# Batch one's forward twiddle tables formed on chip, with full-width forward matmuls and one product per pair

## The chip, the cores and the metric

The kernel runs on one core of one Trainium2 chip. The metric is the device time of one execution in microseconds; for the kernel before it is the median of three runs. The engines are TensorE (PE, with weight loads shown apart as PEld), VectorE (DVE), ScalarE (ACT), GpSimd (POOL) and SyncE (SP). DMAs are issued from the queues of POOL and SP here.

## What is computed

The reference filters a sequence in the frequency domain and sends the result through a small two-layer network with PReLU:

```python
X = np.fft.rfft(x, axis=1)                       # x: 8 batches x 3008 x 256
Y = X * (filt_r + 1j * filt_i)[None]             # 1505 frequencies x 256
y = np.fft.irfft(Y, n=3008, axis=1).reshape(24064, 256)
h = y @ w_in                                     # 256 -> 2048
g = np.maximum(h, 0) + alpha * np.minimum(h, 0)
out = g @ w_out                                  # 2048 -> 256
```

## The kernel before

The FFT of length 3008 is split as 47 x 64. Per batch there are four stages: A (47-point transforms, `piece_a`), B (twiddle and 64-point transform for each of 24 frequencies k1, two to a pair kp, `piece_b`), C (the inverse of B, `piece_c`) and D (the inverse of A, `piece_d`). Between B and C the spectrum is multiplied by the filter. The network works on blocks of up to 512 tokens: `up` (L421 matmuls, ACT copies to `gtb` in L427, DVE does min, multiply and add in L430 and L431) and `down` (L440, stored from L403). All is issued in one hand-written order: a dictionary `plan` says at which step of the blocks' loop each piece of a later batch's transform stands (16 steps a block, from step 0 at the first `up`). Engines work through their queues in order.

Batches 1 to 7 are transformed beside the blocks of earlier batches. Batch 0 (class `First`) comes first, and nothing else can fill TensorE meanwhile. This head is what the change touches:

- The x rows of batch 0 are loaded in four chunks of two DMAs (L139, POOL's queue, with a cast from float32 to float16). `piece_a` runs 16 pieces, four to a chunk; each one's eviction to `am`, a part of `gtb`, alternates between ACT and DVE (L245, L248). `warm` issues matmuls whose results nobody reads.
- The constants follow on POOL's queue in four groups of six frequencies: the forward table `twf_s` (L332), the filter `filt_s` (real and imaginary part, each in a rising and a falling run: four DMAs, L144 and L148), the inverse table `twi_s` (L336) and its crossed copy `twx_s` (L338), which lies in the last three slots of `gtb`. For the first group DVE makes `twx_s` from `twi_s` (`cross`, L354 and L355). Then come `win_s`, `wout_s` and x of batch 1.
- `turn_at` transposes a pair of frequencies into `at` (L278). `piece_b` does eight half-width matmuls (L288) into two banks of a `psH` buffer: one bank has real and imaginary part in one order, the other crossed. DVE multiplies each with the filter (L292, L293) to `uu` and `ww`. `piece_c` sums both through `twi_s` and `twx_s` (L305, L306), ACT evicts to `v`. The order per pair is C of kp, transposes of kp + 3, B of kp + 2.
- `piece_t` (L317) and `piece_d` (L238) finish the batch, its first quarter ahead of the first `up`.

From batch 1 on, `piece_b` takes a 128-wide weight from `twf_s` (L197), DVE multiplies with `filts_s` and `filt_s` (L200, L201), and a DMA adds the halves (L203). For this `filts_s` and `filt_s` have to hold other halves than in batch 0: a DMA after the head (L378), four DVE negations at steps 17, 20, 23 and 26 (`neg`, L481) and a DMA at step 29 bring them there.

PSUM has two `psH` buffers of two banks, two `psO` buffers and two single banks (`psF`), which a string of digits, `BANKS`, deals out.

Of the kernel before, what the change touches and what calls it, by code (L numbers as in the profile page):

```python
# [10 lines left out]
FP16 = mybir.dt.float16  # L11
FP32 = mybir.dt.float32

NFFT = 3008
N1 = 47
N2 = 64
NK1 = 24
D = 256
# [14 lines left out]
AF = mybir.ActivationFunctionType  # L33
OP = mybir.AluOpType


def _build_consts():

    s1 = np.arange(N1)
    s2 = np.arange(N2)
    k1 = np.arange(NK1)
    p = np.arange(64)
    k2 = np.where(p < 32, p, 95 - p)
    g = np.where(p < 32, 1.0, -1.0)

    a1 = 2 * np.pi * np.outer(s1, k1) / N1  # L50
    wf1 = np.zeros((2 * N1, 96))
    wi3 = np.zeros((96, 2 * N1))
    scale = np.where(k1 == 0, 1.0, 2.0) / NFFT
    for h in range(2):
        r = slice(h * N1, h * N1 + N1)
        wf1[r, h * 48 : h * 48 + NK1] = np.cos(a1)
        wf1[r, h * 48 + NK1 : h * 48 + 48] = -np.sin(a1)
        wi3[h * NK1 : h * NK1 + NK1, r] = (np.cos(a1) * scale).T
        wi3[48 + h * NK1 : 48 + h * NK1 + NK1, r] = (-np.sin(a1) * scale).T

    kk = k1[:, None] + 47 * k2[None, :]
    ang = 2 * np.pi * s2[:, None, None] * kk[None, :, :] / NFFT
    c, s = np.cos(ang), np.sin(ang)
    twf = np.empty((128, NK1, 128))
    twf[:64, :, :64], twf[64:, :, :64] = c, s
    twf[:64, :, 64:], twf[64:, :, 64:] = -s * g, c * g
    ec, es = c.transpose(2, 1, 0), s.transpose(2, 1, 0)
    gp = g[:, None, None]
    twi = np.empty((128, NK1, 128))
    twi[:64, :, :64], twi[:64, :, 64:] = ec, es  # L70
    twi[64:, :, :64], twi[64:, :, 64:] = -es * gp, ec * gp
    return wf1, wi3, twf, twi


@with_exitstack
def kernel(
# [8 lines left out]
    out: bass.AP,  # L85
):
    nc = tc.nc
    wf1_np, wi3_np, twf_np, twi_np = _build_consts()
    wf1_d = nc.inline_tensor(wf1_np.astype(np.float16), name="c_wf1")
    wi3_d = nc.inline_tensor(wi3_np.astype(np.float16), name="c_wi3")  # L90
    twf_d = nc.inline_tensor(twf_np.astype(np.float16), name="c_twf")
    twi_d = nc.inline_tensor(twi_np.astype(np.float16), name="c_twi")
    twx_np = np.concatenate([twi_np[64:], -twi_np[:64]])
    twx_d = nc.inline_tensor(twx_np.astype(np.float16), name="c_twx")
    id_d = nc.inline_tensor(np.eye(128, dtype=np.float16), name="c_id")
    wfx_np = wf1_np.reshape(2 * N1, 2, 2, NK1).transpose(0, 3, 2, 1).reshape(2 * N1, 96)
    wfx_d = nc.inline_tensor(np.ascontiguousarray(wfx_np).astype(np.float16), name="c_wfx")
# [15 lines left out]

    wf1_s = konst.tile([2 * N1, 96], FP16, name="wf1_s")
    wi3_s = konst.tile([96, 2 * N1], FP16, name="wi3_s")
    twf_s = konst.tile([128, NK1, 128], FP16, name="twf_s")
    twi_s = konst.tile([128, NK1, 128], FP16, name="twi_s")
    filt_s = konst.tile([128, NK1, D], FP16, name="filt_s")
    filts_s = konst.tile([128, NK1, D], FP16, name="filts_s")
    al16 = konst.tile([16, 128], FP32, name="al16")  # L120
# [40 lines left out]
    class Fft:  # L161
# [31 lines left out]
        def piece_b(self, kp):  # L193
            px = bank().rearrange("p (k d) -> p k d", k=2)
            for kh in range(2):
                k1 = 2 * kp + kh
                nc.tensor.matmul(px[:, kh], twf_s[:, k1], self.at[:, k1], start=True, stop=True)  # L197
            uu = p_uw.tile([128, 2, D], FP16, name="uu", bufs=4)
            ww = p_uw.tile([128, 2, D], FP16, name="ww")
            nc.vector.tensor_mul(ww, px, filts_s[:, 2 * kp : 2 * kp + 2])  # L200
            nc.vector.tensor_mul(uu, px, filt_s[:, 2 * kp : 2 * kp + 2])  # L201
            for o in (0, 64):
                nc.gpsimd.dma_start(out=uu[o : o + 64], in_=ww[64 - o : 128 - o], accum_op=OP.add)  # L203
            self.uw[kp] = (uu,)
# [48 lines left out]
    class First(Fft):  # L253
# [26 lines left out]

        def piece_b(self, kp):
            hp = psH.tile([128, 2, 512], FP32, name="hps")
            px, pz = (hp[:, i].rearrange("p (k d) -> p k d", k=2) for i in range(2))
            for i, ps in enumerate((px, pz)):
                for kh in range(2):
                    k1 = 2 * kp + kh
                    for o in (0, 64):
                        nc.tensor.matmul(ps[o : o + 64, kh], twf_s[:, k1, 64 * i : 64 * i + 64],  # L288
                                         self.at[:, k1], start=True, stop=True)
            uu = p_uw.tile([128, 2, D], FP16, name="uu", bufs=4)  # L290
            ww = p_uw.tile([128, 2, D], FP16, name="ww")
            nc.vector.tensor_mul(uu, px, filt_s[:, 2 * kp : 2 * kp + 2])  # L292
            nc.vector.tensor_mul(ww, pz, filt_s[:, 2 * kp : 2 * kp + 2])  # L293
            self.uw[kp] = uu, ww

        def piece_c(self, kp, evict):
            uu, ww = self.uw.pop(kp)
# [12 lines left out]
        def piece_t(self, i, evict, wide=False):  # L310
# [6 lines left out]
                    nc.tensor.matmul(pt[0:96, o : o + 128], m[:, 8 * f + s // 4, :, s % 4], id16, start=True, stop=True)  # L317
            evict(self.zt[:, 2 * i : 2 * i + 2].rearrange("p a d -> p (a d)"), pt[0:96])

    nc.sync.dma_start(out=id16, in_=id_d.ap())  # L320
    nc.sync.dma_start(out=wfx_s, in_=wfx_d.ap())
    xc = {(0, c): load_x(0, c) for c in range(4)}
    f0 = First()
# [1 line left out]
    nc.sync.dma_start(out=wf1_s, in_=wf1_d.ap())  # L325
    nc.sync.dma_start(out=wi3_s, in_=wi3_d.ap())
    make_identity(nc, id32)
    for g in range(4):
        ka, kb = 6 * g, 6 * g + 6
        kc = slice(ka, 24 if g == 2 else kb)  # L330
        if g < 3:
            nc.gpsimd.dma_start(out=twf_s[:, kc], in_=twf_d.ap()[:, kc])  # L332
        load_filt(filt_s, 0, filt_r, ka, kb)
        load_filt(filt_s, 64, filt_i, ka, kb)
        if g < 3:
            nc.gpsimd.dma_start(out=twi_s[:, kc], in_=twi_d.ap()[:, kc])  # L336
        if g > 0:
            nc.gpsimd.dma_start(out=twx_s[:, ka:kb], in_=twx_d.ap()[:, ka:kb])  # L338
    for kt in range(2):
        nc.gpsimd.dma_start(out=win_s[:, kt], in_=moe_w_in[kt * 128 : (kt + 1) * 128])  # L340
    for q in range(2):
        nc.gpsimd.dma_start(
            out=wout_s[:, 8 * q : 8 * q + 8],
            in_=moe_w_out[1024 * q : 1024 * q + 1024].rearrange("(j p) d -> p j d", p=128))
    for c in range(4):
        xc[(1, c)] = load_x(1, c)

    def warm(n):
        pw = psO.tile([128, 2, D], FP32, name="op")
        for _ in range(n):  # L350
            nc.tensor.matmul(pw[:, 0, 0:128], id16, id16, start=True, stop=True)

    def cross(ka, kb):
        nc.vector.tensor_copy(twx_s[0:64, ka:kb], twi_s[64:128, ka:kb])  # L354
        nc.vector.tensor_scalar(twx_s[64:128, ka:kb], twi_s[0:64, ka:kb], -1.0, None, OP.mult)  # L355

    warm(36)
    for i in range(16):
        f0.piece_a(i, both[i % 2], i % 2 == 1)
        if i % 4 == 3:  # L360
            warm((16, 6, 5, 8)[i // 4])
    alp = psO.tile([128, 2, D], FP32, name="op")
    nc.tensor.transpose(alp[:, 0, 0:16], al16, id32)
    nc.vector.tensor_copy(al_s, alp[:, 0, 0:16])
# [1 line left out]
    f0.turn_at(0, on_act)  # L366
    f0.turn_at(1, on_dve)
    f0.piece_b(0)
    cross(0, 6)
    f0.turn_at(2, on_act)  # L370
    f0.piece_b(1)
    for kp in range(12):
        f0.piece_c(kp, on_act)
        if kp < 9:
            f0.turn_at(kp + 3, on_act)
        if kp < 10:
            f0.piece_b(kp + 2)
    nc.gpsimd.dma_start(out=filts_s[0:64], in_=filt_s[64:128])  # L378
    warm(8)
    for i in range(4):  # L380
        f0.piece_t(i, both[i % 2], i % 2 == 1)
# [7 lines left out]
    for p in range(NB // 2):  # L389
        t = 0  # L390
# [60 lines left out]
    def put(step, fn, *args):  # L451
        plan.setdefault(step, []).append((fn, args))
# [25 lines left out]
            put(d0 + gap * i, f0.piece_d, 4 * g + i, evs[i % len(evs)])  # L478

    def neg(ka, kb):  # L480
        nc.vector.tensor_scalar(filts_s[64:128, ka:kb], filt_s[64:128, ka:kb], -1.0, None, OP.mult)  # L481

    for i in range(4):
        put(17 + 3 * i, neg, 6 * i, 6 * i + 6)
    put(29, lambda: nc.gpsimd.dma_start(out=filt_s[64:128], in_=filt_s[0:64]))
    plan_fft(1, 16, 1, 32, 40, 3, 0, 6, 92, 4, (20, 24, 74, 75))
    plan_fft(2, 66, 2, 97, 109, 4.5, 8, 12, 187, 4, (110, 114, 118, 122))
    for b in range(3, NB):
        p = 96 * (b - 1)
        f = Fft(b)  # L490
# [63 lines left out]
```

## Time and profile before

| what | us |
|---|---|
| median of three runs (796.51 to 797.36) | 796.84 |
| the profiled execution's own time | 795.65 |
| its span, first to last instruction | 793.9 |
| PE / DVE / ACT / POOL busy | 775.0 / 621.2 / 596.9 / 193.2 |
| first x chunk used by `piece_a` | 6.33 |
| last x chunk used | 12.80 |
| first product with the filter starts | 16.34 |
| last of them ends | 33.25 |
| first `up` matmul | 37.81 |
| first `down` matmul | 49.0 |

The page of a profile gives busy times, a strip of 40 slices, DMA queues, the chain of work that ended last, the costliest groups of instructions and DMA issues. In a group's row, "x12 | 8.2, 681" is twelve instructions, 8.2 us busy, 681 ns each on average; behind the next bar is the engine's idle time just before them and what ended it. In the timeline and the chain the first number is the start, the second the length. The span starts at the first instruction. Matmul durations include the pipeline, so one that is listed with 0.22 us can follow its predecessor by 0.06.

### The profile page before, as it was taken

What the parts mean: (1) busy time and instruction counts of PE and PEld (TensorE: products, weight loads), DVE (VectorE), ACT (ScalarE), POOL (GpSimd) and SP (SyncE); (2) the same over time, 40 slices, a digit from 0 to 9 for tenths busy, and PEclk for the clock granted to TensorE, in tenths of its full rate; (3) what the DMA queues carried; (4) which work ended last, traced back from release to release, by engine and by line L of the source; (5) the groups of instructions that cost most, each with busy time, mean ns of one, the idle gap of its engine ahead of it and who ended that gap; (6) DMA issues with size and microseconds to landing.
All of it is one profiled execution on the core that took longest, in us unless ns stands there. A gap on an engine that the chain in (4) does not pass through costs nothing.

```text
span 793.9 us, 16103 instructions
## 1 busy us (share of the span) xinstructions
PE 775.0 (98%) x5956; PEld 538.5 (68%) x5956; DVE 621.2 (78%) x1377; ACT 596.9 (75%) x836; POOL 193.2 (24%) x269
## 2 busy tenths in 40 slices
PE   7999999999999999999999999999999999999997
PEld 6756656666677666766667666766667766766665
DVE  4797985788788787888787877887878888777773
ACT  3788678878778887788768887688867777787663
POOL 7510441153123221341223311242212222000000
PEclk9999999999999999999999999999999999999999
DMA  9967557695776648574684657656494333511111
GB/s 187 209 142 194 115 112 175 192 180 118 150 173 113 138 102 192 123 147 101 149 189 82 135 120 167 152 109 139 101 212 90 66 77 81 138 36 28 41 40 54
DMA packets 102310, 100.58 MB, mean 127 GB/s; under 512 B 11320, under 2 KB 92744, under 8 KB 102104
## 3 DMA queue, kind: packets, MB, share of 16 engines
q1 hardware_dynamic: 79512, 68.80, 32.9%
q0 software_dynamic: 22720, 30.75, 24.3%
q8 instruction: 47, 0.77, 0.4%
q14 instruction: 31, 0.25, 0.1%
HBM read 56.26 MB, written 46.66 MB: 130 GB/s over the span
## 4 chain that ended last, share of the span: by engine, by line
PE 89%; ACT 4%; DMA 3%; DVE 2%; issue 1%; SPq 0%; POOL 0%; ACTq 0%; DVEq 0%; POOLq 0%
PE hps L421 38%; PE op L440 38%; PE psF L177 3%; PE psF L238 3%; ACT gtb L427 2%; PE psF L216 2%; PE psF L197 2%; DMA uu<-ww 1%; DMA filt_s<-in_filt_i_dram 1%; DMA xs<-in_x_dram 1%; ACT asb L245 1%; PE hps L288 1%; PE psF L317 1%; DMA v_dram<-v 0%; DMA zt<-v_dram 0%
## 5 line engine op out<-in xcount | busy, mean ns | idle before, releaser
L427 ACT ACTIVATE gtb<-hps 128x1024 f16<-128x1024 f32 (+1 forms) x384 | 385.4, 1005 | 133.3 <-PE hps L421 127.9
L440 PE MATMUL op<-wout_s,gtb 128*128 128x256 f16 x3008 | 451.1, 272 | 0.6 <-DVE gtb L431 0.6
L421 PE MATMUL hps<-yT,win_s 128*128 128x512 f16 (+1 forms) x1536 | 449.2, 374 | 0.4 <-ACT gtb L427 0.2
L440 PEld LDWEIGHTS <-gtb 128*128 128x128 f16 x3008 | 293.2, 98 | 189.6 <-DVE gtb L431 0.9
L430 DVE TENSOR_SCALAR m<-gtb,alm_s 128x512 f16<-128x512 f16 (+1 forms) x768 | 235.7, 349 | 126.7 <-ACT gtb L427 124.4
L431 DVE TENSOR_TENSOR gtb<-gtb,m 128x1024 f16<-128x1024 f16 (+1 forms) x384 | 261.6, 681 | 19.9
L203 POOL DMA_DIRECT2D uu<-ww x168 | 140.6, 980 | 438.3 <-PE hps L421 322.1
L421 PEld LDWEIGHTS <-win_s 128*128 128x128 f16 x1536 | 145.3, 98 | 30.9 <-issue 3.1
L245 ACT ACTIVATE asb<-psF 96x512 f16<-96x512 f32 x112 | 66.2, 591 | 11.5 <-PE psF L177 11.4
L245 ACT ACTIVATE yT<-psF 128x376 f16<-128x376 f32 x120 | 57.1, 485 | 13.3 <-PE psF L238 12.8
L445 ACT ACTIVATE osb<-op 128x512 f32<-128x512 f32 x96 | 56.1, 585 | 6.1 <-issue 3.2
L245 ACT ACTIVATE v<-psF 128x512 f16<-128x512 f32 x84 | 49.4, 595 | 10.8 <-PE psF L216 10.0
L200 DVE TENSOR_TENSOR ww<-psF,filts_s 128x512 f16<-128x512 f32 x84 | 57.4, 684 | 0.0
L201 DVE TENSOR_TENSOR uu<-psF,filt_s 128x512 f16<-128x512 f32 x84 | 57.2, 681 | 0.0
L139 POOL DMA_DIRECT2D xs<-in_x_dram x64 | 43.9, 946 | 25.8 <-PE psF L177 15.0
L177 PE MATMUL psF<-xs,wf_s 94*96 94x512 f16 x112 | 42.7, 381 | 1.5 <-ACT v L245 1.0
L238 PE MATMUL psF<-wi_s,zt 96*128 96x94 f16 x504 | 40.3, 205 | 1.9 <-DMA zt<-v_dram 1.0
L238 PEld LDWEIGHTS <-zt 96*128 96x128 f16 x512 | 34.3, 97 | 6.2 <-issue 1.5
L216 PE MATMUL psF<-uu,twi_s 128*128 128x256 f16 x168 | 31.3, 273 | 2.3 <-ACT yT L245 0.9
L197 PE MATMUL psF<-at,twf_s 128*128 128x256 f16 x168 | 32.1, 273 | 0.3 <-ACT asb L245 0.2
L216 PEld LDWEIGHTS <-twi_s 128*128 128x128 f16 x168 | 15.7, 98 | 5.9 <-DMA uu<-ww 2.7
L197 PEld LDWEIGHTS <-twf_s 128*128 128x128 f16 x168 | 15.8, 98 | 2.8 <-DVE uu L201 0.7
(55 smaller groups left out, 173.3 us busy)
## 6 DMA issues: line engine op xcount, KB each, us to landing
out_dram<-osb SPq DMA_DIRECT2D x128, 128.0 KB
xs<-in_x_dram POOLq DMA_DIRECT2D x64, 188.0 KB, 5.4
a_dram<-asb SPq DMA_DIRECT2D x28, 384.0 KB
uu<-ww POOLq DMA_DIRECT2D x168, 64.0 KB, 2.9
v_dram<-v SPq DMA_DIRECT2D x112, 96.0 KB
zt<-v_dram SPq DMA_DIRECT2D x28, 384.0 KB
at<-a_dram SPq DMA_DIRECT2D x20, 384.0 KB
at<-a_dram SPq DMA_DIRECT2D x32, 96.0 KB
```

The source lines that it names most:

```text
L177: nc.tensor.matmul(ps[0:96], wf1_s, xs[:, o : o + 512], start=True, stop=True)
L197: nc.tensor.matmul(px[:, kh], twf_s[:, k1], self.at[:, k1], start=True, stop=True)
L200: nc.vector.tensor_mul(ww, px, filts_s[:, 2 * kp : 2 * kp + 2])
L203: nc.gpsimd.dma_start(out=uu[o : o + 64], in_=ww[64 - o : 128 - o], accum_op=OP.add)
L216: nc.tensor.matmul(pv[:, kh], twi_s[:, k1], u[:, kh], start=u is us[0], stop=u is us[-1])
L238: nc.tensor.matmul(ps[:, m], self.zt[:, 8 * g + 4 * mh + m, dh * 128 : dh * 128 + 128], wi3_s, start=True, stop=True)
L245: nc.scalar.activation(o, i, AF.Copy)
L421: nc.tensor.matmul(self.hps[:, j % 2, 0:tn], win_s[:, kt, j * 128 : (j + 1) * 128], yT[:, kt, self.t0 : self.t0 + tn], start=(kt == 0), st ...
L427: nc.scalar.activation(g[:, :, 0:tn], self.hps[:, :, 0:tn], AF.Copy)
L430: nc.vector.tensor_scalar(m[:, i, 0:tn], g[:, i, 0:tn], 0.0, a, OP.min, OP.mult)
L431: nc.vector.tensor_add(g[:, :, 0:tn], g[:, :, 0:tn], m[:, :, 0:tn])
L440: nc.tensor.matmul(self.op[:, si % 2], self.gts[k][:, 128 * si : 128 * si + 128], wout_s[:, k], start=(k == 0), stop=(k == 15))
```

## The change

The forward table is no longer loaded. A base table `rot_s` (128 x 432, float32: cosines, sines and two 192-wide base rows) is loaded ahead of everything on SP's queue, and for each of the 24 frequencies ACT scales one base row and DVE multiplies the other and adds (`gen`), 14 before the evictions of `piece_a` and ten between them. `twf_s` becomes 192 wide per frequency, so that both orders of real and imaginary part are 128-wide windows of it. `piece_b` of batch 0 then needs four full-width matmuls and one product of 1024 elements, with the filter broadcast, written to free slots of `gtb`.

The inverse tables are loaded by half on SP's queue, each load held back by a one-element write of DVE or ACT to its destination, and POOL copies each half to the other partitions (`both_halves`). `cross` is gone. The filter groups are 0 to 4, 4 to 10, 10 to 17 and 17 to 24; the loads of `win_s`, `wout_s` and x of batch 1 stand among or after POOL's copies. The order per pair becomes B of kp + 2, transposes of kp + 4, C of kp − 1. After the head three DMAs set `twi_s` and `filts_s` up for the later batches; the negations now write `filt_s`, and the DMA at step 29 is gone.

```diff
-    twf_s = konst.tile([128, NK1, 128], FP16, name="twf_s")
+    twf_s = konst.tile([128, NK1, 192], FP16, name="twf_s")
+    rot_s = konst.tile([128, 432], FP32, name="rot_s")
...
-                nc.tensor.matmul(px[:, kh], twf_s[:, k1], self.at[:, k1], start=True, stop=True)
+                nc.tensor.matmul(px[:, kh], twf_s[:, k1, 64:192], self.at[:, k1], start=True, stop=True)
...
-                    for o in (0, 64):
-                        nc.tensor.matmul(ps[o : o + 64, kh], twf_s[:, k1, 64 * i : 64 * i + 64],
-                                         self.at[:, k1], start=True, stop=True)
...
-            nc.vector.tensor_mul(uu, px, filt_s[:, 2 * kp : 2 * kp + 2])
-            nc.vector.tensor_mul(ww, pz, filt_s[:, 2 * kp : 2 * kp + 2])
-            self.uw[kp] = uu, ww
+                    nc.tensor.matmul(hp[:, i, D * kh : D * kh + D], twf_s[:, k1, 64 - 64 * i : 192 - 64 * i],
+                                     self.at[:, k1], start=True, stop=True)
+            uw = gtb[:, 6 + kp % 8]
+            f = filt_s[:, 2 * kp : 2 * kp + 2].rearrange("p k d -> p (k d)").unsqueeze(1).to_broadcast([128, 2, 512])
+            nc.vector.tensor_mul(uw, hp, f)
...
+    nc.sync.dma_start(out=rot_s, in_=rot_d.ap())
     nc.sync.dma_start(out=id16, in_=id_d.ap())
...
+    def gen(ka, kb):
+        for k in range(ka, kb):
+            t = p_osb.tile([128, 2, D], FP32, name="osb")[:, 0, 0:192]
+            nc.scalar.activation(t, rot_s[:, 240:432], AF.Copy, scale=rot_s[:, 24 + k : 25 + k])
+            nc.vector.scalar_tensor_tensor(twf_s[:, k], rot_s[:, 48:240], rot_s[:, k : k + 1], t, OP.mult, OP.add)
+
+    def load_twi(ka, kb, ev):
+        ev(twi_s[0:1, ka, 0:1], id16[0:1, 0:1])
+        ev(twx_s[64:65, ka, 0:1], id16[64:65, 0:1])
+        nc.sync.dma_start(out=twi_s[0:64, ka:kb], in_=twi_d.ap()[0:64, ka:kb])
+        nc.sync.dma_start(out=twx_s[64:128, ka:kb], in_=twi_d.ap()[64:128, ka:kb])
+
+    def both_halves(ka, kb):
+        nc.gpsimd.tensor_copy(twi_s[64:128, ka:kb], twi_s[0:64, ka:kb])
+        nc.gpsimd.tensor_copy(twx_s[0:64, ka:kb], twx_s[64:128, ka:kb])
...
+    load_g(0, 4)
+    load_g(4, 10)
+    load_g(10, 17)
...
     warm(36)
+    gen(0, 14)
     for i in range(16):
         f0.piece_a(i, both[i % 2], i % 2 == 1)
         if i % 4 == 3:
             warm((16, 6, 5, 8)[i // 4])
+            gen(*((14, 18), (18, 22), (22, 24), (24, 24))[i // 4])
+        if i == 7:
+            load_twi(0, 4, on_dve)
+        if i == 14:
+            load_twi(4, 12, on_act)
...
     f0.piece_b(0)
-    cross(0, 6)
     f0.turn_at(2, on_act)
     f0.piece_b(1)
+    both_halves(0, 4)
+    load_g(17, 24)
+    both_halves(4, 8)
+    both_halves(8, 12)
+    for kt in range(2):
+        nc.gpsimd.dma_start(out=win_s[:, kt], in_=moe_w_in[kt * 128 : (kt + 1) * 128])
+    load_twi(12, 24, on_act)
+    both_halves(12, 18)
+    both_halves(18, 24)
+    f0.turn_at(3, on_act)
     for kp in range(12):
-        f0.piece_c(kp, on_act)
-        if kp < 9:
-            f0.turn_at(kp + 3, on_act)
         if kp < 10:
             f0.piece_b(kp + 2)
-    nc.gpsimd.dma_start(out=filts_s[0:64], in_=filt_s[64:128])
+        if kp < 8:
+            f0.turn_at(kp + 4, on_act)
+        for k in {9: (8, 9), 10: (10,), 11: (11,)}.get(kp, (kp - 1,) if kp else ()):
+            f0.piece_c(k, on_act)
...
+    nc.gpsimd.dma_start(out=twi_s[64:128], in_=twx_s[64:128])
+    for o in (0, 64):
+        nc.gpsimd.dma_start(out=filts_s[o : o + 64], in_=filt_s[64:128])
...
-        nc.vector.tensor_scalar(filts_s[64:128, ka:kb], filt_s[64:128, ka:kb], -1.0, None, OP.mult)
+        nc.vector.tensor_scalar(filt_s[64:128, ka:kb], filt_s[0:64, ka:kb], -1.0, None, OP.mult)
...
-    put(29, lambda: nc.gpsimd.dma_start(out=filt_s[64:128], in_=filt_s[0:64]))
```

More of the change, by code (lines that the diff above doesn't have):

```diff
@@ L62, in _build_consts @@
     ang = 2 * np.pi * s2[:, None, None] * kk[None, :, :] / NFFT
[L63 to L67, printed above, removed]
+    c, s = np.cos(ang).transpose(2, 1, 0), np.sin(ang).transpose(2, 1, 0)
     gp = g[:, None, None]
     twi = np.empty((128, NK1, 128))
-    twi[:64, :, :64], twi[:64, :, 64:] = ec, es
-    twi[64:, :, :64], twi[64:, :, 64:] = -es * gp, ec * gp
-    return wf1, wi3, twf, twi
+    twi[:64, :, :64], twi[:64, :, 64:] = c, s
+    twi[64:, :, :64], twi[64:, :, 64:] = -s * gp, c * gp
+    phi = 2 * np.pi * np.outer(s2, k2) / N2
+    re, im = np.cos(phi), np.sin(phi)
+    e0 = np.concatenate([np.concatenate([re, -im * g], 1), np.concatenate([im, re * g], 1)])
+    e1 = np.concatenate([np.concatenate([-im, -re * g], 1), np.concatenate([re, -im * g], 1)])
+    base = [np.concatenate([e[:, 64:], e[:, :64], -e[:, 64:]], 1) for e in (e0, e1)]
+    th = 2 * np.pi * np.outer(np.concatenate([s2, s2]), k1) / NFFT
+    rot = np.concatenate([np.cos(th), np.sin(th)] + base, 1)
+    return wf1, wi3, twi, rot
 @with_exitstack
@@ L87 @@
     nc = tc.nc
-    wf1_np, wi3_np, twf_np, twi_np = _build_consts()
+    wf1_np, wi3_np, twi_np, rot_np = _build_consts()
     wf1_d = nc.inline_tensor(wf1_np.astype(np.float16), name="c_wf1")
     wi3_d = nc.inline_tensor(wi3_np.astype(np.float16), name="c_wi3")
-    twf_d = nc.inline_tensor(twf_np.astype(np.float16), name="c_twf")
+    rot_d = nc.inline_tensor(rot_np.astype(np.float32), name="c_rot")
     twi_d = nc.inline_tensor(twi_np.astype(np.float16), name="c_twi")
-    twx_np = np.concatenate([twi_np[64:], -twi_np[:64]])
-    twx_d = nc.inline_tensor(twx_np.astype(np.float16), name="c_twx")
     id_d = nc.inline_tensor(np.eye(128, dtype=np.float16), name="c_id")
@@ L282, in piece_b @@
             hp = psH.tile([128, 2, 512], FP32, name="hps")
-            px, pz = (hp[:, i].rearrange("p (k d) -> p k d", k=2) for i in range(2))
-            for i, ps in enumerate((px, pz)):
+            for i in range(2):
                 for kh in range(2):
                     k1 = 2 * kp + kh
-                    for o in (0, 64):
-                        nc.tensor.matmul(ps[o : o + 64, kh], twf_s[:, k1, 64 * i : 64 * i + 64],
-                                         self.at[:, k1], start=True, stop=True)
[L290 to L293, printed above, removed]
-            self.uw[kp] = uu, ww
+                    nc.tensor.matmul(hp[:, i, D * kh : D * kh + D], twf_s[:, k1, 64 - 64 * i : 192 - 64 * i],
[3 more added lines that the diff above has]
+            nc.vector.tensor_mul(uw, hp, f)
+            self.uw[kp] = tuple(uw[:, i].rearrange("p (k d) -> p k d", k=2) for i in range(2))
         def piece_c(self, kp, evict):
@@ L327, with load_g @@
     make_identity(nc, id32)
[L328 to L332, printed above, removed]
+    def gen(ka, kb):
[11 more added lines that the diff above has]
+        nc.gpsimd.tensor_copy(twx_s[0:64, ka:kb], twx_s[64:128, ka:kb])
+    def load_g(ka, kb):
         load_filt(filt_s, 0, filt_r, ka, kb)
         load_filt(filt_s, 64, filt_i, ka, kb)
[L335 to L346, printed above, removed]
+    load_g(0, 4)
+    load_g(4, 10)
+    load_g(10, 17)
     def warm(n):
@@ L351, in warm @@
             nc.tensor.matmul(pw[:, 0, 0:128], id16, id16, start=True, stop=True)
-    def cross(ka, kb):
-        nc.vector.tensor_copy(twx_s[0:64, ka:kb], twi_s[64:128, ka:kb])
-        nc.vector.tensor_scalar(twx_s[64:128, ka:kb], twi_s[0:64, ka:kb], -1.0, None, OP.mult)
     warm(36)
+    gen(0, 14)
     for i in range(16):
@@ L368 @@
     f0.piece_b(0)
-    cross(0, 6)
     f0.turn_at(2, on_act)
     f0.piece_b(1)
+    both_halves(0, 4)
[8 more added lines that the diff above has]
+    f0.turn_at(3, on_act)
     for kp in range(12):
-        f0.piece_c(kp, on_act)
-        if kp < 9:
-            f0.turn_at(kp + 3, on_act)
         if kp < 10:
             f0.piece_b(kp + 2)
-    nc.gpsimd.dma_start(out=filts_s[0:64], in_=filt_s[64:128])
+        if kp < 8:
+            f0.turn_at(kp + 4, on_act)
+        for k in {9: (8, 9), 10: (10,), 11: (11,)}.get(kp, (kp - 1,) if kp else ()):
+            f0.piece_c(k, on_act)
+    for q in range(2):
+        nc.gpsimd.dma_start(
+            out=wout_s[:, 8 * q : 8 * q + 8],
+            in_=moe_w_out[1024 * q : 1024 * q + 1024].rearrange("(j p) d -> p j d", p=128))
+    for c in range(4):
+        xc[(1, c)] = load_x(1, c)
+    nc.gpsimd.dma_start(out=twi_s[64:128], in_=twx_s[64:128])
+    for o in (0, 64):
+        nc.gpsimd.dma_start(out=filts_s[o : o + 64], in_=filt_s[64:128])
     warm(8)
```

## The prediction

> **What bounds the kernel now.** I read the page first: its busy times and its chain of waits.
>
> ```profile
> PE 775.0 (98%) x5956; PEld 538.5 (68%) x5956; DVE 621.2 (78%) x1377; ACT 596.9 (75%) x836; POOL 193.2 (24%) x269
> PE 89%; ACT 4%; DMA 3%; DVE 2%; issue 1%; SPq 0%; POOL 0%; ACTq 0%; DVEq 0%; POOLq 0%
> ```
>
> TensorE is 98% busy and 89% of the chain. The change leaves the matmuls of the steady part alone, so only the head, where TensorE has gaps, can move the end. Second, busy time by stage:
>
> ```profile
> 10.00:15.00 5.00, 3.29 (x54) 2.83 (x55) 2.70 (x7) 2.01 (x6) 3.24 (x7) 1.00 1.11 250
> 15.00:20.00 5.00, 3.31 (x46) 2.41 (x47) 4.17 (x8) 1.97 (x4) 4.46 (x9) 1.00 1.02 231
> 20.00:25.00 5.00, 5.00 (x78) 3.92 (x75) 4.79 (x8) 3.87 (x9) 4.00 (x8) 1.00 1.11 250
> ```
>
> The columns are length, PE, PEld, DVE, ACT, POOL, clock, DMA share, GB/s. From 10 to 20 us PE is busy two thirds of the time with DMA full; from 20 us PE and DVE both are. Third, the chain of waits of the head:
>
> ```profile
> 9.87 6.34 DMA filt_s<-in_filt_i_dram
> 16.34 0.69 DVE uu L292
> 17.03 0.60 DVE ww L293
> 17.66 0.35 DVE gtb L354
> 18.03 0.36 DVE gtb L355
> ...
> 20.33 0.22 PE psF L278 x4
> 20.55 0.56 PE hps L288 x8
> ...
> 21.73 0.22 PE psF L278 x4
> 21.95 0.56 PE hps L288 x8
> ```
>
> Batch 0's first product waits for a filter load issued at 9.87 us; then come the two cross copies (L354, L355), then a cycle: 28.53 − 20.33 = 8.20 us for six pairs, 1.37 us each. The last product ends at 32.64 + 0.61 = 33.25 us. I count to that point, because from there on the order is the same. Fourth, the groups of the first 50 us kept apart by shape, for durations:
>
> ```profile
> L293 DVE TENSOR_TENSOR ww<-hps,filt_s 128x512 f16<-128x512 f32 x12 | 8.2, 681 | 0.0
> L430 DVE TENSOR_SCALAR m<-gtb,alm_s 128x512 f16<-128x512 f16 x14 | 4.3, 347 | 0.9 <-ACT gtb L427 0.9
> L248 DVE CAST gtb<-hps 128x384 f16<-128x384 f32 x8 | 4.2, 554 | 10.2 <-PE hps L267 10.1
> L245 ACT ACTIVATE gtb<-psF 128x384 f16<-128x384 f32 x8 | 3.6, 489 | 8.4 <-PE psF L267 8.3
> L355 DVE TENSOR_SCALAR gtb<-twi_s 64x768 f16<-64x768 f16 x1 | 0.4, 354 | 0.0
> ```
>
> Fifth, the timeline: VectorE's last eviction of the first stage, and the first negation in the blocks.
>
> ```profile
> 13.34 1.02 DVE L248 CAST gtb<-hps 128x384 f16<-128x384 f32 x2 [1.13 <-PE hps L267]
> 52.59 0.56 DVE L481 TENSOR_SCALAR filts_s<-filt_s 64x1536 f16<-64x1536 f16 x1
> ```
>
> **Part 1: the tables, a cost.** 24 ACT and 24 DVE instructions of 192 float32 elements are put between the evictions of the first stage. DVE: 384 elements took 554 ns and 512 took 681 to 692, so 1.03 ns an element and 155 ns fixed; 192 give 356 ns. A per-partition scalar: L430 took 347 ns; fixed-scalar rows of the same mode (64x768 in 354, L481's 64x1536 in 557) give 287 for 512, so 60 more. That is 416 ns, less the 80 ns by which successive DVE instructions overlap (two casts of 554 in 1.02): 0.33 us each. ACT: 384 elements in 489 ns, 1024 in 1021; 192 give 0.33 us, or 0.24 with the overlap seen there (two of 1021 in 1.94). The three buffers between them allow (0.33 + 0.42 + 0.1 of hand-over) / 3 = 0.28. DVE sets the pace: I take 0.33, bounds 0.24 and 0.42 (no overlap).
>
> Start: the first constant landed at 2.51 us, issued at 0.75. The 221 KB base table now goes ahead of it; by the view of DMA queues, 0.63 MB on that queue took 3.1% of the first 62 us on all engines, so it adds about 0.7 us: 3.2. The first ACT result comes at 3.6, fourteen entries by 8.2 (ACT's evictions began at 6.89 before). Then DVE works without a pause: 8.2, casts 1.02, four entries 1.32, casts, four entries, two tiny copies 0.25, casts, two entries 0.66, casts: 8.2 + 4.08 + 3.30 + 0.25 = 15.8 us, against 14.36 before. The x rows, late by at most the base table's 0.7 us, are there earlier (last chunk used at 12.80). So the first stage ends **1.4 us later**; 0 to 0.6 us at 0.27 an entry or less, where x sets the end, and 3.6 at 0.42.
>
> **Part 2: the filter wait, a gain.** The first group shrinks from six to four frequencies, and the forward table no longer stands before it in the queue. Table and filter (576 KB) took 3.5 us after the last x chunk; 256 KB of filter and 128 KB of inverse table beside it give 2.3, landing at 15.5 behind an x that ends at 13.2. The stage then waits for DVE alone: before, PE had the first pair done at 16.07, 1.7 us after DVE's last cast, 0.27 us before the filter. First product: 15.8 + 1.65 = 17.45, **1.1 us later** than 16.34.
>
> **Part 3: the pairs, a gain.** The cross copies go (0.75 us of DVE). Four full-width matmuls take 4 × 0.11 = 0.44 us (L440's four end 0.33 us after the first) instead of 0.56 for eight halves. One product of 1024: 686 + 512 × 1.04 = 1.22 us, 1.14 in sequence, against 1.37 a pair. It is issued ahead of the rest of its pair, so it waits only for the product two back. PE needs 0.44 + 0.22 + 0.44 = 1.10, ACT two evictions of 0.5 to 0.6. DVE sets 1.14 to 1.20; I take 1.16: 11 × 1.16 + 1.22 = 14.0 us. The last product ends at 17.45 + 14.0 = 31.45, **1.8 us earlier** than 33.25.
>
> **Part 4: the copies on POOL, hidden.** POOL copies the missing halves: 64x512 six times, 64x768 four times, worth 12 of the first. No row shows a POOL copy. Call one P: at least DVE's 0.29 for 512, at most 1.37, twice its one-element rate; I take 0.7, nearest to the 0.69 of a one-element-a-cycle DVE cast. POOL is in order, and each DMA waits for the one eight earlier, as in the trace (0.3 to 1.1 us idle before the issues from 8.06 to 12.94). Twelve filter issues end at 16.2, two copies, then four issues freed by the second filter group (640 KB with the inverse tables beside it, at the 165 KB/us of part 2: 15.5 + 3.9 = 19.4, issued by 20.0); the last copy ends at 20.0 + 4P + 1.2 (win_s issues) + 6P = 21.2 + 10P = 28.2. It is due at the tenth inverse pair, 17.45 + 10 × 1.16 + 1.0 = 30.1. It is hidden while P is under 0.89; each 0.1 us above costs 1.0. [...]
>
> Queued behind on POOL: wout_s, batch 1's x, then the copies to twi_s and filts_s. Bytes up to there are the same (9.8 MB both ways), the queue stays fed, and the last land at about 51, where the one copy landed before (41.85 + 9.1). The first negation now waits for them at 52.59 − 1.8 = 50.8; behind it on DVE stand the second block's min and add, which its down matmuls need 15 steps later, and evictions that free psF banks, of which TensorE finds one more free. That covers 0.2; I charge nothing, bounds 0 and 2.5. The filt_s DMA gone from step 29 had 11 steps of cover and gives nothing.
>
> **Sum.** 1.1 us later into the pairs, 14.0 instead of 16.9 us for them: **−1.8 us**. The bounds are −3.9 (0.24 an entry, x as before, 1.10 a pair: 14.36 + 1.65 + 13.3 = 29.3) and +0.8 (0.42 an entry, 1.20 a pair: 18.0 + 1.65 + 14.4 = 34.05); about 1 us of a waiting negation on top reaches +1.8. Span 793.9 gives 792.1, its own time 795.65 gives 793.85; the median 796.84 lies 1.19 above that, so **795.0**. A measurement here tells 0.2%, 1.6 us, from no change, so this is a narrow win.
>
> **Rivals.**
> (a) Table generation is slower, 0.39 to 0.42 an entry, because ACT reads its scale per partition (60 ns as on DVE) or nothing overlaps. DVE's last cast then ends at 17.2 to 18.0, and of the 1.8 at most 0.4 is left: about 796.6. For it: DVE and ACT alternate, which no row shows. Against: rows with satisfied waits overlap. [...]
> (b) POOL's copies are slow, the slower side. At P = 1.37 the last ends at 34.9, 4.8 us late, each late copy holding an inverse pair on PE and all behind it: −1.8 + 4.8 gives 799.8. It loses the gain at P = 1.07 and is slower by 1.6 from P = 1.23. For it: no row shows P, and the queue is in order. Against: three times DVE's 0.29 us would still pass.
> (c) The negation waits. If the copies land 2.5 us late, DVE (97% busy from 50 to 60) has no room, and banks stay taken: 797.0.
>
> **Chances.** Forecast, 792.9 to 795.2: 0.53; (a) 0.22; (c) 0.10; (b) 0.15. Faster by over 0.2% is the forecast, 0.53; within is (a) and half of (c), 0.27; slower is (b) and the other half of (c), 0.20. The range 792.9 to 798.6 takes in all but most of (b) and a few hundredths below.
>
> **What would show it.** Right: the first-stage casts stretch to near 15.8 with no idle on DVE; products 1.2 us each, 1.14 to 1.2 apart, ending near 31.5; POOL copies near 0.7; the first block's up matmul 1.8 us before 37.81. Wrong: entries 0.4 apart; inverse matmuls idle behind POOL; the first negation behind a DMA; or products waiting for filters.

## The result and the profile after

| | before | after |
|---|---|---|
| median of five runs each, taken together, us | 796.84 (795.76 to 797.36) | 801.79 (800.33 to 803.35) |
| profiled execution: own time / span, us | 795.65 / 793.9 | 800.33 / 798.5 |
| last eviction of the first stage on VectorE ends | 14.36 | 16.13 |
| first product with the filter starts | 16.34 | 18.42 |
| last of them ends | 33.25 | 32.39 |
| first `up` matmul | 37.81 | 37.02 |

The ratio is 1.0067, interval 1.0048 to 1.0086: the change is slower, 795.0 was forecast. The page of the changed kernel, busy times and chain of waits:

```profile
PE 776.6 (97%) x5908; PEld 540.6 (68%) x5908; DVE 627.1 (79%) x1389; ACT 605.7 (76%) x864; POOL 195.1 (24%) x271
PE 83%; DMA 9%; DVE 3%; ACT 2%; issue 1%; POOL 1%; SPq 1%; ACTq 0%; DVEq 0%; POOLq 0%
```

TensorE is as busy as before, but DMA's share of the chain rose from 3 to 9%. To see where, I matched each eviction of an `up` block (L453 now, L427 before) with its counterpart and took the difference of their start times. Negative is earlier than before:

| at, us | 39 to 52 | 56 | 62 to 84 | 300 | 317 | 409 | 503 | 595 to the end |
|---|---|---|---|---|---|---|---|---|
| after − before, us | −0.79 | +2.64 | +4.20 | +3.9 | +4.3 | +4.6 | +4.9 | +5.05 |

(The spans differ by 4.6; every changed kernel below also gets 0.4 to 0.5 us back behind the last block.) So the head did become shorter, by 0.8 us. Between 52 and 62 us 5.0 us are lost, and another 1.15 us in four steps behind 300 us. The chain of waits of that first loss:

```profile
31.08 11.17 DMA xs<-in_x_dram
42.26 0.29 issue
42.55 12.98 DMA filts_s<-filt_s
...
55.62 0.55 DVE filt_s L507
```

The first negation (L507) waits for the second of the two copies to `filts_s`, issued at 42.55 and landed at 55.5. The timeline shows what this does to VectorE and TensorE (behind the operands: idle time before, and what ended it):

```profile
55.62 0.55 DVE L507 TENSOR_SCALAR filt_s<-filt_s 64x1536 f16<-64x1536 f16 x1 [3.85 <-DMA filts_s<-filt_s]
...
58.18 0.38 PE L180 MATMUL psF<-xs,wf_s 94*96 94x512 f16 x1 [3.27 <-DVE zt L251]
58.39 0.60 PE L447 MATMUL hps<-yT,win_s 128*128 128x512 f16 x2
...
59.85 1.06 PE L447 MATMUL hps<-yT,win_s 128*128 128x512 f16 x2
```

VectorE stands still for 3.85 us with an eviction of `zt` queued behind the negation; TensorE, waiting for that bank, stands still for 3.27 us. And the pair of matmuls at 59.85 us takes 1.06 us instead of 0.60. The windows tell why, in the column of the granted clock:

```profile
10.00:15.00 5.00, 3.51 (x64) 3.04 (x63) 4.91 (x15) 4.90 (x14) 3.41 (x7) 0.97 1.10 185
15.00:20.00 5.00, 4.61 (x32) 3.50 (x31) 3.65 (x8) 1.92 (x7) 3.69 (x7) 0.50 1.06 180
20.00:25.00 5.00, 5.00 (x60) 4.47 (x59) 4.94 (x5) 3.93 (x8) 4.74 (x10) 0.85 1.02 194
56.00:58.00 2.00, 0.00 (x0) 0.00 (x0) 1.95 (x5) 0.00 (x0) 0.00 (x0) 1.00 0.79 219
60.00:62.00 2.00, 2.00 (x12) 1.23 (x10) 1.90 (x4) 0.68 (x2) 0.00 (x0) 0.50 0.00 0
```

From 59.1 to 62.5 us the clock was 0.5, which costs another 1.56 us (+2.64 to +4.20). It was 0.5 in the head too, from 14.7 to 21.5; in the kernel before it was 1.0 from 7.9 to 793.0 us. Last in this view: from 10 to 25 us the DMA engines move 185, 180 and 194 GB/s where they had moved 250, 231 and 250, though they are as busy (share 1.10, 1.06 and 1.02, before 1.11, 1.02 and 1.11).

### The profile page after: what moved, and what is told of

It is laid out like the page before. It is cut to its first block, busy times and chain, and to the rows that moved or that the text cites. A ratio compares the mean times of both kernels' runs of the same rounds, so it can differ in the third digit from the quotient of the medians.

```text
span 798.5 us, 16083 instructions
## 1 busy us (share of the span) xinstructions
PE 776.6 (97%) x5908; PEld 540.6 (68%) x5908; DVE 627.1 (79%) x1389; ACT 605.7 (76%) x864; POOL 195.1 (24%) x271
## 4 chain that ended last, share of the span: by engine, by line
PE 83%; DMA 9%; DVE 3%; ACT 2%; issue 1%; POOL 1%; SPq 1%; ACTq 0%; DVEq 0%; POOLq 0%
PE op L466 37%; PE hps L447 36%; PE psF L180 3%; PE psF L241 2%; PE psF L200 2%; PE psF L219 2%; DMA at<-a_dram 2%; DMA filts_s<-filt_s 2%; DMA uu<-ww 2%; DMA xs<-in_x_dram 1%; DVE twf_s L334 1%; ACT gtb L453 1%; DMA gtb<-c_twi 1%; DVE m L456 1%; DMA zt<-v_dram 0%
## 5 line engine op out<-in xcount | busy, mean ns | idle before, releaser
L453 ACT ACTIVATE gtb<-hps 128x1024 f16<-128x1024 f32 (+1 forms) x384 | 385.3, 1004 | 134.2 <-PE hps L447 131.6
L457 DVE TENSOR_TENSOR gtb<-gtb,m 128x1024 f16<-128x1024 f16 (+1 forms) x384 | 261.6, 681 | 19.9
L203 DVE TENSOR_TENSOR ww<-psF,filts_s 128x512 f16<-128x512 f32 x84 | 57.4, 684 | 0.0
L219 PEld LDWEIGHTS <-twi_s 128*128 128x128 f16 x168 | 15.8, 98 | 5.8 <-DMA uu<-ww 2.5
```

The costliest lines, as they stand in the source:

```text
L219: nc.tensor.matmul(pv[:, kh], twi_s[:, k1], u[:, kh], start=u is us[0], stop=u is us[-1])
L453: nc.scalar.activation(g[:, :, 0:tn], self.hps[:, :, 0:tn], AF.Copy)
L457: nc.vector.tensor_add(g[:, :, 0:tn], g[:, :, 0:tn], m[:, :, 0:tn])
```

## The experiments

**The theories.** W: the loss is the first negation's wait for `filts_s<-filt_s` and the half clock behind it; it comes from where those two DMAs stand in POOL's queue, and goes when the negations come later or the DMAs earlier. Its rivals, in the expectations, put the loss on the half clock of the head, on the forming of the table, or on something spread over the steady part. The kernel before ran again beside each group of experiments: medians 797.57 (e1 to e4), 797.13 (e5 to e8) and 797.02 us (e10 to e13). The ratios are against these.

**e1, late negations.**

```diff
-        put(17 + 3 * i, neg, 6 * i, 6 * i + 6)
+        put(28 + 3 * i, neg, 6 * i, 6 * i + 6)
```

> The changed kernel with the four negations of filt_s at steps 28, 31, 34 and 37 instead of 17, 20, 23 and 26; nothing else differs. Theory W (the first negation's wait for the filts_s DMAs held VectorE 3.85 us and through it TensorE 3.3 us, and TensorE then ran 3.4 us at half clock): both go, the lead of 0.79 us that the changed kernel had at step 12 is kept, and the time is 796 to 797.2 (4.5 to 5.8 us under the changed kernel). Theory S (the steady part itself got slower, by the 192-wide table rows or by what follows the head on the queues, and the wait only stood where time would have been lost anyway): the time stays within 1.5 us of the changed kernel, 800 or more.

Measured: 796.39 us (12 runs), ratio 0.9988 (0.9976 to 1.0). The wait and the half clock at 59 us are gone, the lag stays at −0.56 from 40 to 90 us. But it creeps to +1.51 at the end, 1.35 of it in one step at 498 us. W holds for the 5 us; something else takes 2.

**e2, the two copies ahead of batch 1's last x loads**, negations where the change has them.

```diff
     for c in range(4):
+        if c == 2:
+            for o in (0, 64):
+                nc.gpsimd.dma_start(out=filts_s[o : o + 64], in_=filt_s[64:128])
         xc[(1, c)] = load_x(1, c)
     nc.gpsimd.dma_start(out=twi_s[64:128], in_=twx_s[64:128])
-    for o in (0, 64):
-        nc.gpsimd.dma_start(out=filts_s[o : o + 64], in_=filt_s[64:128])
```

> The changed kernel with the two filts_s DMAs issued between batch 1's second and third x chunk, and the twi_s DMA left behind the fourth; the negations stay at step 17. Theory W, with the place in the queue as the cause: two x chunks of 2.1 us and 393 KB of twi_s (1.8 us) no longer stand ahead, filts_s lands at about 49.5 instead of 55.5, before the negation at 51.8, and the third and fourth chunk, used from steps 24 and 28 on, still land in time at 52 to 55: 796 to 797.2, as with late negations. If instead the two DMAs take that long whatever stands ahead of them (64 rows of 12 KB each), they land at 53 or later and 1 to 4 us of the wait stay: 798 to 800. Theory S: 800 or more.

Measured: 796.11 us (12 runs), 0.998 (0.9969 to 0.999). Its first negation, in the timeline, stands where it stood in the changed kernel's program and waits for nothing (no bracket):

```profile
51.86 0.55 DVE L508 TENSOR_SCALAR filt_s<-filt_s 64x1536 f16<-64x1536 f16 x1
```

So it is the copies' place in the queue, not the negations themselves. The same creep is there: −0.72 early, +1.48 at the end.

**e3, more warming matmuls in the head** (on e1).

```diff
-            warm((16, 6, 5, 8)[i // 4])
+            warm((24, 16, 19, 24)[i // 4])
```

> Late negations as in e1, and 24, 16, 19 and 24 unread matmuls behind the four chunks of the first stage instead of 16, 6, 5 and 8. Theory C (TensorE's idle time between the chunks lets the granted clock fall to 0.5 from 14.7 to 21.5 us, and the first transposes and forward matmuls at half speed start the first product 0.64 us later): the clock stays at 1.0, the first product starts at 17.7 to 17.9 instead of 18.4, and the time is 0.5 to 0.7 us under e1. Rival: the half clock has no cost because VectorE sets the pace; then the first product moves by under 0.2 us and the time is that of e1 within 0.3 us.

Measured: 796.78 us (12 runs), 0.9987 (0.9977 to 0.9998). The first product's four matmuls, in the changed kernel and then in e3:

```profile
17.37 1.01 PE L289 MATMUL hps<-at,twf_s 128*128 128x256 f16 x4 [0.26 <-ACT at L248]
```

```profile
17.41 0.60 PE L289 MATMUL hps<-at,twf_s 128*128 128x256 f16 x4 [0.46 <-ACT at L248]
```

The clock is 1.0 throughout, the first product starts at 18.05 instead of e1's 18.65, and the lead at 40 to 84 us is 1.47 instead of 0.56. So the half clock did cost the head, 0.9 us in this pair; in two more pairs below (e8 and e5, e11 and e7) it is 1.1 and 0.3. But 0.5 of the 0.9 is gone by 89 us, where batch 1 comes in, and the median isn't lower than e1's.

**e4, the 192-wide table loaded instead of formed** (on e1): POOL's queue brings it in, a part ahead of each filter group.

```diff
-            gen(*((14, 18), (18, 22), (22, 24), (24, 24))[i // 4])
...
-    gen(0, 14)
...
-    rot_s = konst.tile([128, 432], FP32, name="rot_s")
...
     def load_g(ka, kb):
+        nc.gpsimd.dma_start(out=twf_s[:, ka:kb], in_=twf_d.ap()[:, ka:kb])
```

> Late negations as in e1, and the 192-wide forward table loaded on POOL's queue ahead of each filter group instead of being formed: no base table, no ACT and DVE instructions for it, 0.96 MB more to load. If forming the table costs what I charged (first stage 1.4 to 1.8 us longer), VectorE's last cast ends at 14.4 to 14.9 instead of 16.1. The first product then waits for table and filter of the first group, at about 16.4, 2 us earlier than 18.4. If the load is what forming saves, later groups come late: the products wait for filters and the last ends later than 32.4, time 0 to 3 us above e1. If loading is no worse, the last product ends near 30.5 and the time is 1 to 2 us under e1.

Measured: 794.92 us (10 runs), 0.9964 (0.9952 to 0.9977). The pairs end hardly earlier than with the formed table (32.44 against 32.61 us in e1), and one product now waits 0.5 us for a filter load. The gain is elsewhere: the lag is −0.73 early and −0.43 at the end, **without the creep**. Either forming causes the creep, or something that went with it. One such thing: `rot_s` takes 1728 bytes a partition, 192 above a multiple of 256, and so moves all buffers declared behind it (`at`, `asb`, `zt`, `v`, `xs`) from addresses of 128 modulo 256, as in the kernel before, to 64.

**e5, e7: the formed table with other addresses** (on e1). In e5 448 makes it 1792 bytes (the buffers are at 128 modulo 256 again); e7 has 480 in the same place, 1920 bytes (0 modulo 256).

```diff
-    rot_s = konst.tile([128, 432], FP32, name="rot_s")
+    rot_s = konst.tile([128, 448], FP32, name="rot_s")
...
-    nc.sync.dma_start(out=rot_s, in_=rot_d.ap())
+    nc.sync.dma_start(out=rot_s[:, 0:432], in_=rot_d.ap())
```

> The kernel with the late negations, with one edit: rot_s is declared 1792 bytes a partition instead of 1728, the 64 bytes unused, so that every buffer declared behind it (at, asb, zt, v, xs) begins at 128 modulo 256 bytes, as in the kernel before, and not at 64. Theory P (the second loss is a matter of where the DMA buffers lie): the 512-byte packets of at<-a_dram fall from 37.7 ns to 36.7 ns, the first forward matmuls of batches 4 to 7 wait under 0.05 us more than in the kernel before, the lag behind the kernel before changes by under 0.3 us from 100 us to the end, and the ratio is 0.997 (0.9955 to 0.998), where e1 gave 0.9988. Theory F (it comes with the forming, or differs from one execution to the next): packets 37.7 ns, waits of 0.15 to 1.3 us at 312, 403, 498 and 590 us, 1.5 us lost over the run, ratio 0.9988.

> As the kernel with 1792 bytes, but 1920 bytes: the buffers begin at 0 modulo 256 bytes. Theory P with 64 bytes as the unit that is lost: packets of at<-a_dram at or under 36.7 ns, no waits, ratio as with 1792 bytes (0.997); if a boundary of 256 or 512 bytes is what costs, packets are shorter still (under 36 ns) with the time the same, since nothing waits for them any more. Theory F: as e1, packets 37.7 ns and 0.9988.

**e6: the loaded table with the old shift** (on e4), the reverse.

```diff
+    gap_s = konst.tile([128, 432], FP32, name="gap_s")
+    nc.gpsimd.memset(gap_s[:, 0:1], 0.0)
```

> The kernel with the loaded table, with one edit: a tile of 1728 bytes a partition that nothing uses (one column is set to zero) stands where rot_s stood, so that the buffers behind it begin at 64 modulo 256 bytes. Nothing else changes. Theory P: packets of at<-a_dram 37.7 ns instead of 36.6, waits of TensorE for at<-a_dram at the first forward matmuls of batches 4 to 7 (about 312, 403, 498, 590 us) of 1 to 2.5 us together, ratio 0.998 to 0.999 where e4 gave 0.9964. Theory F: no wait there, packets 36.6 ns, ratio 0.9964 (0.995 to 0.9975).

Measured: e5 794.46 us (10 runs), 0.9966 (0.9954 to 0.9978); e7 794.09 (6 runs), 0.9965 (0.9953 to 0.9978); e6 797.56 (12 runs), 1.0001 (0.9989 to 1.0012). P holds both ways: 64 unused bytes bring 2 us, and a tile that nothing uses costs e4 2.6. The line of SP's DMA queue (packets, MB, share of 16 engines' span) on the pages of e4, e6 and e7:

```profile
q1 hardware_dynamic: 79992, 69.59, 33.3%
```

```profile
q1 hardware_dynamic: 79992, 69.59, 33.7%
```

```profile
q1 hardware_dynamic: 80136, 69.81, 31.9%
```

With the spans 793.1, 794.6 and 792.2 that is 52.8, 53.6 and 50.5 ns a packet. For the 512-byte packets of that queue alone, over the whole execution, the trace has 34.9 ns in e4 and e5 (35.1 before), 36.1 in e6 (36.2 in the changed kernel) and 32.9 in e7. (The expectations' 37.7 and 36.7 are not these means; the order is the same.) The waits of TensorE at L203 of e6 are the creep:

```profile
PE psF L203 <- DMA at<-a_dram: 0.6, 3, 0.2
```

They stand at 402, 497 and 589 us (one more of 0.2, at 310, has no releaser), at the first forward matmuls of batches 4 to 7. The lag steps up by 0.3 to 0.4 at each, 1.4 together, of which the recorded waits are 0.8. Of the traces of all kernels here, the five at 64 have such waits (0.4 to 1.2 us in all), the five at 0 have none, and of the four at 128 only e5 has one. That one is a miss: I expected e5's waits gone, and its profiled execution waits 0.6 us, at 498 us. That execution took 796.73 us, the slowest of its ten, so at 128 the load was late in that one; the profiles of the kernel before, e4 and e8 show it in time.

**e8, e11: late negations, fuller warming and 128 or 0 modulo 256 together** (e11 has 480 for the 448 of e8).

```diff
-            warm((16, 6, 5, 8)[i // 4])
+            warm((24, 16, 19, 24)[i // 4])
...
-    rot_s = konst.tile([128, 432], FP32, name="rot_s")
+    rot_s = konst.tile([128, 448], FP32, name="rot_s")
```

> The late negations, the 1792 bytes, and the fuller warming calls (24, 16, 19 and 24 matmuls instead of 16, 6, 5 and 8) together. If the three effects add up: clock 1.0 throughout the head, first product at 18.05 us, lead over the kernel before of 1.47 us at 84 us and no loss of more than 0.3 us behind it save the 0.5 us at 89 us: 795.4 to 796.0 as profiled against 796.84 and a ratio of 0.9965 (0.995 to 0.998). If the second loss remains: 0.9987 as e3.

> Late negations, fuller warming calls, and 1920 bytes. Lead over the kernel before of 1.4 us at 84 us, as with 1792 bytes; if what that kernel lost at 89 us (0.8 us) depends on the addresses, the lead stays, and the time is 793.3 to 793.9, ratio 0.9958; if it does not, 794.4 and 0.9967, no better than without the fuller warming calls (0.9965).

Measured: 794.66 us (5 runs), 0.9969 (0.9957 to 0.9981), and 794.63 (10 runs), 0.997 (0.9959 to 0.9981). Their leads at 84 us, 1.38 and 1.15, shrink to 0.57 and 0.50 at 89 us. What stands there in the timeline, in e7 and then in e8, is the first inverse matmul of batch 1:

```profile
84.10 0.39 PE L219 MATMUL psF<-uu,twi_s 128*128 128x256 f16 x2 [0.57 <-DMA uu<-ww]
```

```profile
84.74 0.39 PE L219 MATMUL psF<-uu,twi_s 128*128 128x256 f16 x2 [1.70 <-DMA uu<-ww]
```

The matmul waits for the DMA that adds the halves, and in e8 it starts later than in e7 although all ahead of it was earlier. What a shorter head gains beyond e7 is given back at this wait, whatever the addresses (1.54 us in e11, 1.43 in e3). What holds that DMA up wasn't tried.

**e10: the changed kernel, only the addresses mended** (0 modulo 256).

```diff
-    rot_s = konst.tile([128, 432], FP32, name="rot_s")
+    rot_s = konst.tile([128, 480], FP32, name="rot_s")
```

> The changed kernel with one edit: rot_s takes 1920 bytes a partition instead of 1728, so that the buffers behind it begin at 0 modulo 256 bytes; the negations stay where the change has them. If the two losses are separate and add up: the wait of the first negation for filts_s<-filt_s stays at 3 to 4.5 us, the half clock behind it too, the lag behind the kernel before is +4.0 to +4.4 us at 70 us and doesn't grow behind 130 us; 794.1 (late negations at the same addresses) + 5.0 = 799.1 us, ratio 1.0030 (1.0010 to 1.0045). If the addresses also make the 12-KB rows of filts_s<-filt_s faster, the wait is shorter by as much. If the addresses do nothing: 1.0067, as the changed kernel.

Measured: 799.16 us (12 runs), 1.0024 (1.0012 to 1.0037); 799.1 was expected. The negation still waits, nearly as long as in the changed kernel:

```profile
55.52 0.55 DVE L507 TENSOR_SCALAR filt_s<-filt_s 64x1536 f16<-64x1536 f16 x1 [3.53 <-DMA filts_s<-filt_s]
```

The lag is +4.06 at 70 us and has no step behind 138 us. The two losses are separate, and the addresses don't speed up the copies (the second one took 12.98 us from issue to landing in the changed kernel and 12.95 here).

**e12: the kernel before at 0 modulo 256.** Does it gain as well?

```diff
+    gap_s = konst.tile([128, 32], FP32, name="gap_s")
+    nc.gpsimd.memset(gap_s[:, 0:1], 0.0)
```

> The kernel before with one edit: a tile of 128 bytes a partition that nothing uses (one column is set to zero), so that the buffers behind it begin at 0 modulo 256 bytes. The kernel before shows no wait for at<-a_dram, so shorter packets have nothing to shorten: ratio 1.000 (0.999 to 1.001), packets of at<-a_dram on their queue 32.9 ns instead of 35.1. If it is faster by over 0.2%, a part of the gain of the late negations with 1920 bytes (0.9965) is owed to the addresses alone and not to the change.

Measured: 797.85 us (12 runs), 1.0015 (1.0001 to 1.0028), packets 32.9 ns. Not faster: what e7 gains on the kernel before is the change's own. Its profiled execution, at 800.33 us one of the slowest of the twelve, shows the same wait for `uu<-ww`, 2.0 us at 87 us with half clock behind it; the kernel before had 0.9 us there, for another cause. Whether that is the addresses or chance I can't say.

**e13: the loaded table, fuller warming, 0 modulo 256** (on e4).

```diff
-            warm((16, 6, 5, 8)[i // 4])
+            warm((24, 16, 19, 24)[i // 4])
...
+    gap_s = konst.tile([128, 32], FP32, name="gap_s")
+    nc.gpsimd.memset(gap_s[:, 0:1], 0.0)
```

> The table loaded instead of formed, late negations, fuller warming calls, addresses at 0 modulo 256 bytes. Nothing is formed, so the last cast ends at 14.5 to 15.1 us and the first product starts at 16.2 to 16.8, 1.3 us earlier than with the formed table; but the loaded table lies ahead of the filters in the queue, and the product of pair 5 waits for its filters until about 25 us, so the last product ends at 31.5 to 33.0 all the same: 0.9955 to 0.9975, within 0.1% of the same kernel with the formed table. If the filters do not hold it up, the last product ends at 30.0 and the time is 1.7 us lower than with the formed table.

Measured: 796.17 us (12 runs), 0.9986 (0.9975 to 0.9997), worse than I gave it. The products in its timeline, with the pauses between:

```profile
18.42 5.75 DVE L296 TENSOR_TENSOR gtb<-hps,filt_s 128x1024 f16<-128x1024 f32 x5 [0.37 <-PE hps L292]
25.84 3.49 DVE L296 TENSOR_TENSOR gtb<-hps,filt_s 128x1024 f16<-128x1024 f32 x3 [1.66 <-PE op L309]
29.64 4.61 DVE L296 TENSOR_TENSOR gtb<-hps,filt_s 128x1024 f16<-128x1024 f32 x4 [0.32 <-PE op L309]
```

The chain there runs `twf_s<-c_twf`, then `filt_s<-in_filt_i_dram`, issued at 22.40 and landed at 29.5, where the last four products begin. Two other delays came on top: the 24 unread matmuls held TensorE from 15.11 to 16.61 us while the last cast had ended at 15.99, and in the first pause an inverse matmul waited 1.13 us for a copy of POOL. So this run alone doesn't tell what the load costs. At equal addresses the formed table had the lower median in all three pairs: by 0.5 us (e5 and e4), 1.2 (e1 and e6) and 1.5 (e11 and e13); only the last pair ran in one group. Forming the table isn't idle work: it takes the table out of the queue that the filters come through.

## Why the prediction was wrong, step by step

All medians, by where the buffers lie modulo 256 bytes:

| kernel | 64 | 128 | 0 |
|---|---|---|---|
| before | not run | 796.84 | 797.85 |
| the change | 801.79 | not run | 799.16 |
| late negations (e1, e5, e7) | 796.39 | 794.46 | 794.09 |
| late negations, table loaded (e6, e4) | 797.56 | 794.92 | not run |

Reading down, the negation's wait costs 5.1 to 5.4 us; reading across, the addresses cost the changed kernels 1.9 to 2.6, while the kernel before gained nothing at 0. The table mixes groups in which the kernel before had 796.84 to 797.57 us, so a difference between groups is uncertain by some 0.7. Without both losses the change is worth 0.35% (e7), 794.09 us. That this lies near the 795.0 that I forecast is in part luck: in e7's trace the head gives a lead of 0.9 us, not 1.8, and the rest of the gain comes from elsewhere.

- **The step that failed** is in part 4: "Bytes up to there are the same (9.8 MB both ways), the queue stays fed, and the last land at about 51", with the conclusion that the negation costs nothing, bounds 0 and 2.5. The bytes were the same (9.88 and 9.93 MB by the packets), and the DMA engines stayed busy, but for a dip worth 0.4 us from 24 to 26 us (share 0.76 and 0.86). But equal bytes did not take equal time. The last load of batch 1's x and the copies from SBUF to SBUF behind it, first before and then after (in the rows of copies: KB each, median us from issue to landing):

```profile
40.97 0.51 POOL L139 DMA_DIRECT2D xs<-in_x_dram  x1 [1.97 <-DMA wout_s<-in_moe_w_out_dram]
filts_s<-filt_s POOLq DMA_DIRECT2D x1, 768.0 KB, 9.1
```

```profile
40.10 0.51 POOL L142 DMA_DIRECT2D xs<-in_x_dram  x1 [3.28 <-DMA wout_s<-in_moe_w_out_dram]
twi_s<-gtb POOLq DMA_DIRECT2D x1, 384.0 KB, 8.1
filts_s<-filt_s POOLq DMA_DIRECT2D x2, 768.0 KB, 12.1
```

That x load landed 7.4 us after its issue before, at 48.4, and 7.3 us after it now, at 47.4. So 1.1 MB less ahead of it brought the queue forward by only 1.0 us. What had gone was table rows of some KB; the 512-byte pieces of the filter stayed (from 10 to 25 us 3.65 MB in 2369 packets before, 2.79 MB in 2700 now). Behind the x load stood one copy, done 2.6 us later; now three stand there, 1920 KB instead of 768, done 8.1 us later (at 49.1, 52.7 and 55.5). These 5.5 us more, less the 1.0, are the 4.5 us by which the last copy came late. POOL's copies of the table halves did put back its issues (`wout_s` to 28.27 from 25.92, batch 1's first x to 30.04 from 27.68), but not the landing (the second half of `wout_s` at 39.8 instead of 40.7). That the place behind the loads decides is shown by e2; the split into 1.0 and 5.5 is read from the two traces.
- **Its price.** Rival (c) had the mechanism, with copies 2.5 us late. They were 4.5 late, the wait was 3.85, and I reckoned nothing for what TensorE's 3.27 us of idleness do to the granted clock: 1.56 us more. The half clock lasts 3.4 us, from 59.1 to 62.5, and begins 0.9 us after TensorE went to work again at 58.18. In e1 and e2, without the wait, the clock is 1.00 from 50 to 70 us.
- **The addresses** weren't in the sum at all, and cost 1.9 to 2.6 us. I took a new tile for its DMA and its arithmetic, not for what it pushes aside. The premise that "only the head, where TensorE has gaps, can move the end" failed twice: the larger loss stands at 52 to 62 us, this one behind 300.
- **Part 1**, 0.33 us an entry: 4.91 / 14 = 0.35. DVE's 416 ns were right (415), ACT took 442 and not 330. The last cast ended at 16.13, with 15.8 forecast. So a small share of rival (a) came true.

```profile
L293 DVE TENSOR_TENSOR gtb<-hps,filt_s 128x1024 f16<-128x1024 f32 x12 | 13.9, 1217 | 0.7 <-DMA filt_s<-in_filt_r_dram 0.6
L333 ACT ACTIVATE osb<-rot_s 128x192 f32<-128x192 f32 x24 | 8.9, 442 | 1.2 <-DMA rot_s<-c_rot 1.2
L334 DVE SCALAR_TENSOR_TENSOR twf_s<-rot_s,osb 128x192 f16<-128x192 f32 x24 | 8.4, 415 | 3.8 <-ACT osb L333 3.7
L343 POOL COPY twi_s<-twi_s 64x512 f16<-64x512 f16 x3 | 1.8, 606 | 1.4 <-DMA twi_s<-c_twi 1.2
```

- **Part 2**: the filter wait went, as said; the first group's loads landed by 14.8. (The first row gives 0.6 us to a filter load. It had long landed: the matmuls ended at 18.38, 0.04 ahead of the product.) But from the last cast to the first product it took 2.29 us and not 1.65, at half clock; e3, at full clock, took 1.83.
- **Part 3**: 1.217 us a product, 1.13 apart at full clock and 1.28 at half, 13.97 us in all against 14.0. Right. With parts 1 and 2 late by 0.97 the head gained 0.8 us and not 1.8.
- **Part 4, POOL's copies**: 606 ns for 512 elements, 0.7 taken; the last ended at 28.32, with 28.2 forecast, and no inverse pair waited. Rival (b) is out.

Not settled: the profiled executions of the five kernels at 64 show 1.2 to 1.9 us of steps behind 300 us, and the medians differ by up to 2.6. The rest may lie in executions like e5's that are late now and then; no profile here shows it.

## What to carry to other kernels

Follow the last DMA of a rebuilt queue to its landing by what each kind of transfer takes, not by equal bytes (here 9.88 and 9.93 MB landed 4.5 us apart), and look at what stands behind the first instruction that waits for it; here 3.3 us of idle TensorE cost half as much again in clock. When a change adds a tile, look at the addresses of all buffers behind it, and pad it to a multiple of 256 bytes, so that these stay where they were, before the change is judged; here e5's 64 unused bytes brought 1.9 us. Work taken off one queue can pay by what is then no longer in front of something else: here the formed table had medians 0.5 to 1.5 us below those of the loaded one.

## What the runs showed of the hardware

- 512-byte packets between DRAM and SBUF took 32.6 to 33.1 ns where the SBUF buffers begin at 0 modulo 256 bytes (five traces), 34.7 to 35.1 at 128 (four) and 35.7 to 36.2 at 64 (five); e6 (36.1) has four waits at the first forward matmuls of batches 4 to 7, e7 (32.9) and e4 (34.9) have none. Why 64 is slower than 128 was not shown.
- Copies from SBUF to SBUF in rows of 6,144 and 12,288 bytes, with hardly anything else moving, went at 221 GB/s over all 16 engines in the changed kernel (the second number from the end is their share, the last the rate):

```profile
46.00:50.00 4.00, 3.96 (x24) 2.13 (x22) 3.90 (x11) 3.34 (x5) 0.00 (x0) 1.00 1.02 221
```

- In the head the clock fell to 0.5 from 14.7 to 21.5 us though TensorE was busy for 3.51 of the 5 us from 10 to 15, more than in the kernel before (3.29), where it stayed at 1.0; e3 kept it with 4.37 of 5. Even e4 and e6, which differ only in an unused tile, had 0.5 from 13.1 to 19.9 us and 1.0 throughout. A busy share doesn't tell it, so more filling is only worth trying, not counting on.
